# Joint attention scores as two 288-key pieces with a full-height mask matmul, and the third group's attention ordered ahead of weight splitting

## The chip, the cores and the metric

The kernel runs on one core of a Trainium2 chip. The time is device microseconds of that core for one execution, the median of several. An execution that was recorded by the hardware profiler gives the trace; its span is counted from the first instruction to the last.

## What is computed

Causal attention with a decay, for 4 batches of 8 heads (576 positions, 64 numbers per head), and behind it two gated expert layers on the 2304 positions:

```python
def _attn_ref(q, k, v, f):                      # [4, 8, 576, 64], f: [4, 8, 576]
    scores = np.matmul(q, k.transpose(0, 1, 3, 2)) / np.sqrt(D)
    cum = np.cumsum(np.log(np.clip(f, 0.0001, 1.0)), axis=-1)
    scores = np.where(causal, -1e9, scores + cum[:, :, :, None] - cum[:, :, None, :])
    attn = np.exp(scores - np.max(scores, axis=-1, keepdims=True))
    return np.matmul(attn / (np.sum(attn, axis=-1, keepdims=True) + 1e-09), v)

x = attn_out.transpose(0, 2, 1, 3).reshape(2304, 512)
xn = x / np.sqrt(np.mean(x * x, -1, keepdims=True) + 1e-06) * rms_g
x = (silu(xn @ w_gate) * (xn @ w_val)) @ w_out          # 512 -> 1536 -> 512
return (silu(x @ w_gate2) * (x @ w_val2)) @ w_out2
```

## The kernel before

**Precision.** Numbers that need more than one pass are kept as a rounded high part and a remainder (called hi and lo). A product in the expert layers is three matmuls: hi by hi, hi by lo, lo by hi (lines 1758 to 1760). Splitting a 128x512 weight tile is a cast on ScalarE or VectorE (lines 307 and 309) and a subtraction on GpSimd or VectorE (line 312).

**Groups.** The 2304 positions are worked on in four groups of 512 to 640. Groups 1 and 2 (`GROUPS` with kind 0) hold the first 256 positions of the batches, groups 3 and 4 (kind 1) the remaining 320 of batches 0, 1 and of 2, 3. While the expert layers of one group run on TensorE, the attention of the next one is worked in between: group 3's beside the expert layers of group 2 (from 278.8 us), group 4's beside those of group 3 (from 544.3 us). The last group's expert layers are computed with a seven-product scheme (from line 1380 and 1472 on).

**Weights.** A group's expert layers use 72 weight tiles, 12 matmuls of 512 columns each. The first group converts them, splits them and stores the unsplit ones. The second group's `fetch` loads them again, splits them, and stores the split form to memory (the DMA on line 1735); the third group loads the split form (line 1727). Eleven tiles are there at most at a time, so loads and splits run ahead of TensorE by as many.

**One pair of heads of kind 1** (`pair_wide`, `wide_part`). Two heads are worked on together in three parts. Part 0 has 128 queries against 384 keys, part 1 the next 128 against 512, each head in a PSUM bank of its own. Part 2, the *joint* part, has the last 64 queries of both heads, 64 rows for each, against all 576 keys: the operands of one head are zero in the rows of the other, and both accumulate into the same bank. Since a bank holds 512 columns, the keys go in two pieces, 512 and 64. Each piece is four matmuls, for each of two heads a 128-row one (line 810: hi and lo of queries against hi of keys) and a 68-row one (line 811: remainders and decay). At the end of a part a mask matmul adds a large negative number above the diagonal: a constant triangle times the identity, accumulated onto the last 128 columns (line 817) or, in the joint part, onto the 64-column piece, where only 64 rows of the constants are used (line 815).

Then VectorE takes the maximum of each piece (line 828) and of the two, ScalarE the exponential with its sum (line 846), one of three engines the scaling (867, 869), TensorE the transposes (919), ScalarE or VectorE the split of the transposed weights (307, 309, 931), and TensorE the product with the values (947). A pair's keys and queries are loaded and split before that by `head_kq` (616 to 626 and 307, 312), its values by `head_v`.

**What sets the order.** The program is written out by a list scheduler (`Plan`) before it runs. Each piece of work is a generator with a priority; the scheduler estimates when every next operation could start on each engine, and takes the one with the earliest start; among those within 0.01 us of each other the lowest priority number goes first. The order on each engine is then fixed. Priorities: weights 2 plus the tile's number times 0.0001 (`W_PRIO`); attention `A_PRIO`, one number for each half of each group (the third group's are the fifth and sixth: 2.5 and 4.2), its loads and splits 0.2 lower; evacuation of expert layers near 0; expert matmuls 5 and more. A pair of the third group may start when the second group's expert layers have reached a given tile (`UNIT_SPREAD`: the first head at tile 4 and one every 4 tiles, the second half from tile 32).

**What the change touches.** The constant `A_PRIO` (line 88), and in `wide_part` the plan of pieces (792), the mask matmul (815), the slices of the exponentials (840, 845). The tile `dC`, which takes the exponentials, has 576 columns before and after.

Of the kernel before, what the change touches and what calls it, by code (L numbers as in the profile page):

```python
# [17 lines left out]
B, H, S, D = 4, 8, 576, 64  # L18
# [17 lines left out]
NCH = (2, 5)  # L36
NMAX = max(QN)
NW, NL = 512, 384

COLS = ((0, 256), (0, 256), (128, 448), (0, 320))  # L40
LEFT_OVER = COLS[2][0] + NW
# [43 lines left out]
H_PSUM = [lambda h: h % 4 == 0, lambda h: True, lambda h: True]  # L85
MB = 2
W_PRIO = 2
A_PRIO = (3, 4, 4.1, 4.1, 2.5, 4.2, 4.2, 0.5)
W_FREE = 0
A16, D16, S16 = 0.885, 0.485, 0.485  # L90
W_EARLY, W_FIRST = 4.5, 7
# [140 lines left out]
def pe(n):  # L232
    return max(0.107, n / 2400 + 0.0135)
# [18 lines left out]
def actp(n):  # L252
    return n / 1200 + 0.168
# [10 lines left out]
def op(eng, dur, fn, *deps):  # L264
    return Op(((eng, dur, 0.0),), lambda e: fn(), deps)
# [12 lines left out]
def tile_attention_moe_moe(  # L278
# [13 lines left out]
    nc = tc.nc  # L292
# [43 lines left out]
    mir = sb.tile([P, 4, P], F32R, name="mir")  # L336
# [418 lines left out]
    def pair_wide(hds, before, started, done):  # L755


        hd = hds[0]
        kind, s = hd.kind, hd.slots
        yield wait(before, hds[0].kq_ready, hds[1].kq_ready)  # L760
        st, e0 = yield Take(s["tm"], ())
        hl, e1 = yield Take(s["p"], (e0,))
        scored, scaled, split_, out_ = [], [], [], [[], []]
        n = 3 if kind else 2
        ev = [{x: Event() for x in ("scored", "scaled", "split")} for _ in range(n)]
        for i in range(n):
            spawn(wide_part(hds, i, st, hl, ev[i], Event(max(e0.t, e1.t))), plan.current[1])
        yield wait(*(x["scored"] for x in ev))
        last = Event(max(x["scored"].t for x in ev))
        for x in hds:  # L770
            x.kq_drop(last)
        later(started, last)
        yield wait(*(x["scaled"] for x in ev))
        s["tm"].give(st, Event(max(x["scaled"].t for x in ev)))
        both_ = []
        for i, x in enumerate(hds):
            both_.append(Event())
            spawn(wide_values(x, i, hl, [e for y in ev for e in (y["split"],)], both_[i], done[i]), plan.current[1])
        yield wait(*both_)
        s["p"].give(hl, Event(max(e.t for e in both_)))  # L780

    def wide_part(hds, part, st, hl, ev, e0):
        hd = hds[0]
        kind, s = hd.kind, hd.slots
        joint = part == 2
        kn = ((128, 256), (384, 512, 576))[kind][part]
# [2 lines left out]
        tok, e1 = yield Take(sc_tokens[hd.style], ())  # L789

        if joint:
            plan_ = (((0, 1), 0, 512, 0),), (((0, 1), 512, D, 0),)
        elif kind:
            plan_ = (((0,), 0, kn, 0),), (((1,), 0, kn, 0),)
        else:
            plan_ = (((0,), 0, kn, 0), ((1,), 0, kn, kn)),
        sc, es = [], []
        for groups in plan_:
            bank, eb = yield Take(banks, ())

            def mm():
                for heads, k0, m, col in groups:
                    o = bank[:, col : col + m]
                    first = True
                    for x in heads:
                        k1, kb, q1, qb = hds[x].kq
                        qs = slice(320 - D * x, 448 - D * x) if joint else slice(q0, q0 + P)
                        ks = slice(k0, k0 + m)
                        last = k0 + m < kn and x == heads[-1]
                        nc.tensor.matmul(o, q1[:, qs], k1[:, ks], start=first, stop=False)  # L810
                        nc.tensor.matmul(o, qb[:, qs], kb[:, ks], start=False, stop=last)  # L811
                        first = False
                    if k0 + m == kn:
                        if joint:
                            nc.tensor.matmul(o, mir[:D, 3], mir[:D, 1, :D], start=False, stop=True)
                        else:
                            nc.tensor.matmul(bank[:, col + kn - P : col + kn], mir[:, 0], mir[:, 1], start=False, stop=True)

            cost = sum(2 * len(h) * pe(m) for h, _, m, _ in groups) + pe(P)
            e = yield op("PE", cost, mm, hds[0].kq_ready, hds[1].kq_ready, e0, e1, eb)  # L820
            sc.append(bank)
            es.append(e)
        later(ev["scored"], es[-1])
        c = 8 * part
        for i, (bank, e) in enumerate(zip(sc, es)):
            if kind:
                m = plan_[i][0][2]
# [8 lines left out]
        dt, e1 = yield Take(s[("dA", "dB", "dC")[part]], ())  # L836
        ex = []
        for i in range(2):
            if joint:
                o, src, b = dt[:, 512 * i : 512 + D * i], sc[i][:, : (512, D)[i]], 0  # L840
            else:
                o, b = dt[:, kn * i : kn * (i + 1)], i
                src = sc[i][:, :kn] if kind else sc[0][:, kn * i : kn * (i + 1)]
            ex.append((yield op(
                "ACT", actp(kn if not joint else (512, D)[i]) + 0.3,
                lambda: nc.scalar.activation(
                    o, src, AF.Exp, scale=0.125, bias=st[:, c + 2 + b : c + 3 + b], accum_out=st[:, c + 4 + i : c + 5 + i]
                ), em, e1,
            )))
            if kind:  # L850
                banks.give(sc[i], ex[i])
# [10 lines left out]
        for i in range(k):  # L862
            o, m = dt[:, w // k * i : w // k * (i + 1)], st[:, c + 4 + i : c + 5 + i]
# [701 lines left out]
    def attention(g):  # L1565

        for s in range(2):
# [4 lines left out]
            for h, hd in enumerate(heads):  # L1572
# [3 lines left out]
                early = () if g == 0 or at < 0 else (steps[g - 1][max(at - 6, 0)],)  # L1576
                pr = A_PRIO[2 * g + s] + i * 0.001
                if hd.style:
# [426 lines left out]
```

## Time and profile before

| | |
|---|---|
| median of 3 runs | 1082.31 us (1080.14 to 1084.54) |
| profiled execution, span | 1078.3 us (its time outside the span isn't recorded; the median is 4.0 above) |
| instructions | 17640, of them 5584 matmuls |
| VectorE, ScalarE, GpSimd busy | 780.6, 602.4, 452.3 us |
| memory traffic | 193.31 MB read, 86.65 MB written, 260 GB/s |
| granted TensorE clock | 0.995 of 2.4 GHz in the mean |

Matmuls are pipelined: the profile gives each one a duration (0.39 us for 512 columns) that is longer than the distance to the next one's start (0.23 us), and its ends are modelled. What a matmul costs in a row of matmuls is therefore read from the starts. A row `L810 PE MATMUL bank<-k,q 128*128 128x512` is a matmul of line 810 with 128 rows of contraction, 128 columns of weights and a moving operand of 512 columns.

### The profile page before, as it was taken

What the parts mean: (1) busy time and instruction counts of PE and PEld (TensorE: products, weight loads), DVE (VectorE), ACT (ScalarE), POOL (GpSimd) and SP (SyncE); (2) the same over time, 40 slices, a digit from 0 to 9 for tenths busy, and PEclk for the clock granted to TensorE, in tenths of its full rate; (3) what the DMA queues carried; (4) which work ended last, traced back from release to release, by engine and by line L of the source; (5) the groups of instructions that cost most, each with busy time, mean ns of one, the idle gap of its engine ahead of it and who ended that gap; (6) DMA issues with size and microseconds to landing.
All of it is one profiled execution on the core that took longest, in us unless ns stands there. A gap on an engine that the chain in (4) does not pass through costs nothing.

```text
span 1078.3 us, 17640 instructions
## 1 busy us (share of the span) xinstructions
PE 1068.1 (99%) x5584; PEld 943.6 (88%) x5584; DVE 780.6 (72%) x1634; ACT 602.4 (56%) x1326; POOL 452.3 (42%) x484
## 2 busy tenths in 40 slices
PE   8999999999999999999999999999999999999998
PEld 8888888888888888888888888888889999999998
DVE  6878888888455657776647766777776878788773
ACT  6776768775556664776325565555643335543352
POOL 0321302324356666658325774657823340244310
PEclk9989999999999999999999999999999999999999
DMA  7846799775997776775899899997895557755583
GB/s 212 259 163 219 265 310 309 231 257 161 366 399 258 241 243 228 252 248 205 303 374 363 303 347 377 340 339 264 326 333 168 196 186 244 234 179 169 193 260 109
DMA packets 136497, 281.21 MB, mean 261 GB/s; under 512 B 14674, under 2 KB 57490, under 8 KB 136402
## 3 DMA queue, kind: packets, MB, share of 16 engines
q1 hardware_dynamic: 136404, 280.09, 75.7%
q8 instruction: 44, 0.72, 0.3%
q14 instruction: 49, 0.40, 0.1%
HBM read 193.31 MB, written 86.65 MB: 260 GB/s over the span
## 4 chain that ended last, share of the span: by engine, by line
PE 96%; DMA 1%; DVE 1%; POOL 1%; issue 0%; ACT 0%; POOLq 0%; DVEq 0%; SPq 0%
PE bank L1758 18%; PE bank L1759 18%; PE bank L1760 18%; PE bank L1472 5%; PE bank L1474 5%; PE bank L1473 5%; PE bank L947 3%; PE bank L919 3%; PE bank L1381 3%; PE bank L1382 3%; PE bank L1380 3%; PE bank L810 2%; PE bank L811 2%; PE bank L667 2%; PE bank L720 2%; PE bank L704 1%
## 5 line engine op out<-in xcount | busy, mean ns | idle before, releaser
L312 POOL TENSOR_TENSOR whl<-w,whl 128x512 fp32r<-128x512 f32 x119 | 157.8, 1329 | 216.4 <-ACT whl L307 170.3
L1758 PE MATMUL bank<-X,whl 128*128 128x512 f32 x564 | 227.3, 403 | 0.0
L1759 PE MATMUL bank<-X,whl 128*128 128x512 f32 x564 | 220.7, 391 | 0.0
L1760 PE MATMUL bank<-X,whl 128*128 128x512 f32 x564 | 220.3, 391 | 0.0
L307 ACT CAST whl<-w 128x512 fp32r<-128x512 f32 x178 | 108.7, 617 | 38.5 <-PE bank L1759 15.5
L1760 PEld LDWEIGHTS bank<-X,whl 128*128 128x128 f32 x564 | 106.2, 188 | 23.3
L1758 PEld LDWEIGHTS bank<-X,whl 128*128 128x128 f32 x564 | 106.3, 188 | 20.6
L1759 PEld LDWEIGHTS bank<-X,whl 128*128 128x128 f32 x564 | 106.5, 189 | 18.9
L1758 PE MATMUL bank<-H,whl 128*128 128x512 f32 x215 | 87.4, 407 | 0.0
L1760 PE MATMUL bank<-H,whl 128*128 128x512 f32 x215 | 84.9, 395 | 0.0
L1759 PE MATMUL bank<-H,whl 128*128 128x512 f32 x215 | 84.9, 395 | 0.0
L1900 ACT ACTIVATE tmp<-bank 128x384 f32<-128x384 f32 x48 | 23.6, 492 | 92.0 <-DVE bank L1510 91.2
L1890 ACT ACTIVATE tmp<-bank 128x512 f32<-128x512 f32 x72 | 43.1, 599 | 50.6 <-PE bank L1760 49.4
L1892 DVE SCALAR_TENSOR_TENSOR tmp<-tmp,bank 128x512 f32<-128x512 f32 x72 | 49.3, 684 | 25.4 <-ACT tmp L1890 23.6
L1913 DVE SCALAR_TENSOR_TENSOR bank<-tmp,bank 128x512 f32<-128x512 f32 x60 | 41.6, 694 | 32.5 <-PE bank L1760 32.3
L312 DVE TENSOR_TENSOR whl<-w,whl 128x512 fp32r<-128x512 f32 x78 | 54.5, 705 | 11.8 <-ACT whl L307 11.1
L828 DVE TENSOR_REDUCE tm<-bank 128x1 f32<-128x512 f32 (+1 forms) x96 | 50.4, 560 | 15.0 <-PE bank L811 7.9
L931 DVE TENSOR_TENSOR pl<-bank,ph 128x512 fp32r<-128x512 f32 (+1 forms) x80 | 49.9, 631 | 8.7 <-ACT ph L307 8.3
L1695 POOL TENSOR_SCALAR w<-w,rebase 128x512 f32<-128x512 f32 x19 | 18.0, 951 | 88.3 <-DMA w<-w 84.1
L1712 DVE SCALAR_TENSOR_TENSOR w<-w,wk 128x512 int32<-128x512 int32 x72 | 52.9, 742 | 1.4 <-ACT wk L1701 1.1
L312 POOL TENSOR_TENSOR kb<-raw,k 64x576 fp32r<-64x576 f32 x31 | 44.4, 1432 | 19.5 <-ACT k L307 18.1
L1473 PE MATMUL bank<-X,whl 128*128 128x384 f32 x154 | 51.4, 334 | 0.0
(306 smaller groups left out, 2815.9 us busy)
## 6 DMA issues: line engine op xcount, KB each, us to landing
whl<-w_split SPq DMA_DIRECT2D x90, 512.0 KB
w<-w SPq DMA_DIRECT2D x72, 512.0 KB
w<-w_f SPq DMA_DIRECT2D x144, 256.0 KB
w_split<-whl SPq DMA_DIRECT2D x72, 512.0 KB
w_f<-w SPq DMA_DIRECT2D x72, 256.0 KB
w_sums<-w SPq DMA_DIRECT2D x48, 256.0 KB
w_sums_split<-whl SPq DMA_DIRECT2D x23, 512.0 KB
w<-w_sums SPq DMA_DIRECT2D x41, 256.0 KB
```

The source lines that it names most:

```text
L307: nc.scalar.copy(o, i)
L312: (nc.vector if e == "DVE" else nc.gpsimd).tensor_tensor(o, a, b, op=ALU.subtract)
L828: em = yield op("DVE", dve(m), lambda: nc.vector.tensor_reduce(st[:, c + i : c + i + 1], bank[:, :m], axis=AX.X, op=ALU.max), e)
L931: e = yield op("DVE", dve(n), lambda: nc.vector.tensor_tensor(low, src, o.bitcast(F32), op=ALU.subtract), e)
L1472: nc.tensor.matmul(o, w[:, 0, cs], xh, start=c == 0, stop=False)
L1473: nc.tensor.matmul(o, w[:, 0, cs], xl, start=False, stop=False)
L1474: nc.tensor.matmul(o, w[:, 1, cs], xh, start=False, stop=c == 1)
L1712: lambda: nc.vector.scalar_tensor_tensor(ti, ti, 3, k, op0=ALU.logical_shift_left, op1=ALU.bitwise_or), e, et,
L1758: nc.tensor.matmul(o, wh[:, cs], xh, start=start, stop=False)
L1759: nc.tensor.matmul(o, wh[:, cs], xl, start=False, stop=False)
L1760: nc.tensor.matmul(o, wl[:, cs], xh, start=False, stop=stop)
L1892: "DVE", dve(n), lambda: nc.vector.scalar_tensor_tensor(a, a, 1.0, b, op0=ALU.add, op1=ALU.mult), e,
```

## The change

The joint part's two pieces become equal: 288 and 288 keys. The mask matmul uses all 128 rows of the constants (the identity's rows from 64 on are zero in the 64 columns used, so these rows add nothing) and is accumulated onto the last 64 columns of the second piece. Maximum and exponential are taken of 288 columns twice. The third group's attention gets the priority 1.9 in both halves, below the weights' 2.

```diff
+JOINT = S // 2
-A_PRIO = (3, 4, 4.1, 4.1, 2.5, 4.2, 4.2, 0.5)
+A_PRIO = (3, 4, 4.1, 4.1, 1.9, 1.9, 4.2, 0.5)
@@ wide_part
-            plan_ = (((0, 1), 0, 512, 0),), (((0, 1), 512, D, 0),)
+            plan_ = (((0, 1), 0, JOINT, 0),), (((0, 1), JOINT, JOINT, 0),)
...
-                            nc.tensor.matmul(o, mir[:D, 3], mir[:D, 1, :D], start=False, stop=True)
+                            nc.tensor.matmul(o[:, m - D :], mir[:, 3], mir[:, 1, :D], start=False, stop=True)
...
-                o, src, b = dt[:, 512 * i : 512 + D * i], sc[i][:, : (512, D)[i]], 0
+                o, src, b = dt[:, JOINT * i : JOINT * (i + 1)], sc[i][:, :JOINT], 0
...
-                "ACT", actp(kn if not joint else (512, D)[i]) + 0.3,
+                "ACT", actp(JOINT if joint else kn) + 0.3,
```

## Rows read from the trace of the kernel before

**Rows 1.** The page: busy us of each engine, share of the span, instructions.

```profile
PE 1068.1 (99%) x5584; PEld 943.6 (88%) x5584; DVE 780.6 (72%) x1634; ACT 602.4 (56%) x1326; POOL 452.3 (42%) x484
```

**Rows 2.** The page: the chain that ended last, by engine.

```profile
PE 96%; DMA 1%; DVE 1%; POOL 1%; issue 0%; ACT 0%; POOLq 0%; DVEq 0%; SPq 0%
```

**Rows 3.** Waits of TensorE: for whom, us in total, times, longest.

```profile
...
PE bank L919 <- POOL dB L869: 1.1, 1, 1.1
PE bank L919 <- POOL dA L869: 0.4, 1, 0.4
...
```

**Rows 4.** Line 815: count, duration in ns, first and last start, forms.

```profile
L815 PE MATMUL bank<-mir x16: 294/294/294, 320.5 to 769.7; 64*128 64x64 f32 x16
```

**Rows 5.** Timeline of TensorE, one joint part: start us, us, instruction.

```profile
692.01 0.39 PE L810 MATMUL bank<-k,q 128*128 128x512 f32 x1
...
692.47 0.40 PE L810 MATMUL bank<-k,q 128*128 128x512 f32 x1
...
692.94 0.20 PE L810 MATMUL bank<-k,q 128*128 128x64 f32 x1
...
693.09 0.28 PE L810 MATMUL bank<-k,q 128*128 128x64 f32 x1
693.20 0.28 PE L811 MATMUL bank<-kb,qb 68*128 68x64 f32 x1
693.40 0.29 PE L815 MATMUL bank<-mir 64*128 64x64 f32 x1
...
693.96 0.39 PE L1759 MATMUL bank<-X,whl 128*128 128x512 f32 x1
694.19 0.39 PE L1760 MATMUL bank<-X,whl 128*128 128x512 f32 x1
```

**Rows 6.** Timeline of TensorE, parts 0 and 1 of the same pair.

```profile
687.12 0.33 PE L810 MATMUL bank<-k,q 128*128 128x384 f32 x1
...
687.48 0.22 PE L817 MATMUL bank<-mir 128*128 128x128 f32 x1
...
689.46 0.40 PE L1759 MATMUL bank<-X,whl 128*128 128x512 f32 x1
```

**Rows 7.** Groups by shape, lines 828 and 846: busy us, mean ns, idle before.

```profile
L828 DVE TENSOR_REDUCE tm<-bank 128x1 f32<-128x512 f32 x48 | 32.6, 683 | 8.0 <-PE bank L811 7.9
L828 DVE TENSOR_REDUCE tm<-bank 128x1 f32<-128x384 f32 x32 | 16.4, 549 | 7.0 <-PE bank L817 7.0
...
L828 DVE TENSOR_REDUCE tm<-bank 128x1 f32<-128x64 f32 x16 | 3.4, 213 | 0.0
...
L846 ACT ACTIVATE dC<-bank,tm 128x512 f32<-128x512 f32 x16 | 11.1, 693 | 0.2 <-DVE tm L835 0.2
...
L846 ACT ACTIVATE dC<-bank,tm 128x64 f32<-128x64 f32 x16 | 5.0, 311 | 0.0
```

**Rows 8.** Tile dC: its transposes, first and last start.

```profile
L919 PE MATMUL bank<-mi,dC x80: 270/272/273, 328.5 to 780.4; 128*128 128x128 f32 x64, 128*64 128x128 f32 x16
```

**Rows 9.** Line 1735: the stores of split weights, first and last start.

```profile
L1735 SPq DMA_DIRECT2D w_split<-whl x72: 319/327/1312, 272.5 to 520.0; - x72
```

**Rows 10.** Timeline of TensorE where the second and third group's expert layers begin.

```profile
278.77 0.39 PE L1758 MATMUL bank<-X,whl 128*128 128x512 f32 x1
...
543.60 0.40 PE L1758 MATMUL bank<-late_h,whl 128*128 128x512 f32 x1
...
544.30 0.40 PE L1758 MATMUL bank<-X,whl 128*128 128x512 f32 x1
```

**Rows 11.** Groups of GpSimd by shape from 278 to 545 us: preparation of heads.

```profile
L312 POOL TENSOR_TENSOR kb<-raw,k 64x576 fp32r<-64x576 f32 x15 | 21.4, 1427 | 5.8 <-ACT k L307 5.5 <-DMA w_split<-whl 0.2
L312 POOL TENSOR_TENSOR v<-rv,v 128x320 fp32r<-128x320 f32 x16 | 14.2, 890 | 5.3 <-ACT v L307 4.9
L312 POOL TENSOR_TENSOR q<-raw,q 64x256 fp32r<-64x256 f32 x16 | 11.9, 746 | 4.6 <-ACT q L307 3.5
```

**Rows 12.** Stretch of the third group's expert layers: busy us by engine, PEclk, DMA.

```profile
545.00:812.00 267.00, 265.44 (x1325) 223.01 (x1324) 189.89 (x426) 144.04 (x352) 153.90 (x180) 1.00 0.93 335
```

## The prediction

> **What bounds the kernel now.** I read the page's busy line first. TensorE has a matmul in flight for 99% of the span, the next engine for 72% [rows 1]. Matmul ends are modelled, so I asked next whether the starts wait for anything. The chain of waits says no: 96% of it is matmul following matmul [rows 2]. Of the few entries in the list of what matmuls waited for, two lie in the stretch in which the joint parts run, 1.1 and 0.4 us, both for a scaling on GpSimd [rows 3]. So from the second group on, the time is the sum of the steps from one matmul's start to the next, and an edit is worth what it takes out of these steps, as long as it makes no new wait.
>
> **The change, part by part.** The joint part runs 16 times (its mask matmul on line 815 is counted 16 times, from 320.5 to 769.7 us [rows 4]).
>
> *The joint part's length now.* I take it from its first matmul to the second expert matmul behind it, because a short matmul shifts part of its cost into the step after the next start. 692.01 to 693.96 is 1.95 us; one step of an undisturbed 512-column matmul (693.96 to 694.19, 0.23) belongs to the expert matmul, so the joint part holds TensorE for 1.72 us [rows 5]. Inside it: a pair of 512-column matmuls, one with 128 rows and one with 68, steps 0.46 to 0.47 (692.01 to 692.47 to 692.94). The 64-column matmuls step 0.11 each (693.09 to 693.20), although they have an eighth of the columns. Two pairs at 0.47 and four at 0.11 make 1.38, and the mask matmul on 64 rows is left with 0.34: 0.20 before it starts (693.20 to 693.40) and a late follower.
>
> *The price of a mask matmul of full height.* The two parts before the joint one hold two pairs of 384 columns, two pairs of 512 and four full-height masks of 128 columns. From 687.12 to the second expert matmul at 689.46 it is 2.34, less 0.23, so 2.11 [rows 6]. A 384 pair takes 0.36 (687.12 to 687.48), a 512 pair 0.47; 2.11 - 0.72 - 0.94 = 0.45, or 0.11 per mask, the same as a 64-column matmul [rows 5, 6].
>
> *Mask edit.* 0.34 becomes 0.11: 0.23 less, 16 times, 3.7 us. A full-height mask of 64 columns has no row. It may be as cheap as nothing, wholly hidden behind its neighbours, or as dear as the present 0.34. I take 0.11, since the two nearest kinds agree on it.
>
> *Score edit.* Two 512 pairs and two 64 pairs become four pairs of 288 columns. No row has 288. From 384 columns (0.36) to 512 (0.47) a pair grows by 0.11 in 128 columns; 96 columns fewer than 384 take off 0.08, so I take 0.28. The bounds: a pair can't be cheaper than two 64-column steps (0.22), nor dearer than a 384 pair (0.36). Four pairs: 1.12 (0.88 to 1.44) against 1.38 now, so 0.26 less, 16 times 4.2 us (between 8.0 gained and 1.0 lost).
>
> *Sum.* 1.72 - (1.12 + 0.11) = 0.49 us each, 16 x 0.49 = 7.8 us. With both ends of both prices: from -1.0 (dear pairs, mask unchanged) to 8.0 + 16 x 0.34 = 13.4 us.
>
> A rule of the Trainium skill speaks against the score edit: in "TensorE: Matmul & The Clock Gate", section "Back-to-back issue gap", a warm isolated matmul is put at N/2.4 + 2.5 ns. Both versions stream 2304 columns in eight score matmuls, so by it the edit is worth nothing and the sum is 3.7. The trace is near it at 512 columns (0.23 us [rows 5] against 0.216) and far off at 64 (0.11 against 0.029), so I go by the trace.
>
> *VectorE and ScalarE.* Reduce and exponential are split 288 + 288 instead of 512 + 64. Reduces take 0.683, 0.549 and 0.213 us for 512, 384 and 64 columns; exponentials 0.693 and 0.311 for 512 and 64 [rows 7]. Both are close to straight lines in the columns, so two of 288 cost what 512 and 64 cost together (0.896 and 1.004): nothing, and neither engine is the bound. What moves is the order inside: the last reduce, which runs when TensorE has left the part, grows from 0.21 to some 0.43 (between the 64 and 384 rows). So the joint part's weights are ready 0.2 us later against TensorE. That is covered: from the mask at 320.5 [rows 4] to the first transpose of these weights at 328.5 [rows 8] lie 8 us of other matmuls, and no wait on them stands in the list [rows 3].
>
> *The order edit.* The third group's attention (eight pairs of heads) goes ahead of the weight splitting on ScalarE, VectorE, GpSimd and the DMA queue. The list scheduler decides by it only between pieces that could start within 0.01 us of each other. Its gain: TensorE doesn't wait in that stretch, so nothing. Its cost: split weights come later. The first is sent to its store at 272.5 [rows 9] and used at 278.8 [rows 10], 6.3 us of lead; the last is stored at 520.0 [rows 9] and its 12 matmuls, at 0.233 each (543.60 to 544.30 are three), end at 544.30 [rows 10], so it is used from 541.5, with 21 us of lead. A head's preparation puts 1.43 + 0.89 + 0.75 = 3.1 us on GpSimd [rows 11], 6.2 us for a pair; were a split to stand behind a whole pair, it would still be in time, and with VectorE (72% busy [rows 1]) as the second engine for splits. I cost it at nothing. If the cover is gone, it shows at the first pairs, by 2 to 5 us in all. The loads of heads and weights share one queue, issued in the scheduler's order; in the busiest stretch, behind 545 us, the 16 DMA engines are at 0.93 [rows 12] and the shorter joint parts squeeze that by 8 x 0.49 of 267 us, 1.5%, to 0.94, which still holds. The waits of 1.1 and 0.4 may go or return elsewhere: 1.5 us either way.
>
> **The sum against the times.** 1078.3 of span less 7.8 is 1070.5. The runs' median of 1082.3 lies 4.0 above the span; that stays, so I predict 1074.5 us.
>
> **Rivals.**
> 1. *Columns alone set the steps* (the rule above as a mechanism of this kernel: the 0.11 of a 64-column step is an effect of this place, not of its size, and comes back in the 288 steps). Only the mask edit pays: 1082.3 - 3.7 = 1078.6. For it: 288 has no row. Against it: the steps of 0.11 [rows 5]. 5%.
> 2. *The mask stays dear* because what costs is its place at the end of a group, not its 64 rows. Then 1082.3 - 4.2 = 1078.1. Against it: full-height masks close a group too, at 0.11 [rows 6]. 5%.
> 3. *The order edit and the new plan make waits.* TensorE's order is fixed beforehand; a transpose that meets a scaling not yet done stops everything behind it. One such wait is 1.1 us [rows 3]; four or five more give back 5 us: 1079.5. For it: every queue's order from the second group on is planned anew. Against it: only two such waits among 16 pairs now. 10%.
> 4. *Slower.* The same stop, but built into the joint part: if the later second reduce lets the transposes of dC come before their scaling in all 16 parts, at 1.1 us each it is 17.6 us, and 1082.3 - 7.8 + 17.6 = 1092.1. It eats the gain from seven such parts on, and is a measurable loss from 12. Against it: the 8 us of other matmuls between [rows 4, 8]. 6%.
> 5. *More than forecast*: pairs near 0.24 (16 x 4 x 0.04 = 2.6 us more) and both present waits gone (1.5): 1070.4. 6%.
>
> **How the numbers follow.** The forecast has the remaining 68%, with its own range 1072 to 1077 (a pair between 0.25 and 0.31, waits 1.5 up or down). A measurement of this kernel can tell 0.5%, 5.4 us, from no change, so faster means below 1076.9: the forecast nearly whole (66%), case 5 (6%), a fifth of case 3: 74%. Within 0.5%: cases 1 and 2, most of 3, the edge of the forecast: 20%. Slower: 6%. The range 1070 to 1079.5 leaves out case 4 and some of 3 and 5.
>
> **What would show it.** Lines 810 and 811 should have only 288-column forms in the joint part, 64 matmuls on each line, stepping 0.28 a pair; the joint part should hold TensorE for 1.2 us by the same reading; the mask should be a 128-row form and its follower start within 0.1. The span should lose what the 16 parts lose. The prediction is wrong if a 288 pair steps 0.32 or more, if the expert matmul behind the mask still comes 0.3 late, or if the list of TensorE's waits between 280 and 812 us grows past 4 us; a first split weight that TensorE waits for soon after 278.8 us would convict the order edit.

## The result and the profile after

Five runs of each, the changed kernel at a median of 1069.59 us (1067.01 to 1071.79), the kernel before at 1082.31 (1075.94 to 1085.31): ratio 0.9914, interval 0.9886 to 0.9942. The ratio is the record's own estimate with its 95% interval; the quotient of these two medians is 0.988, just outside it, and the record doesn't show what makes the difference. Measured again in a later set the ratio was 0.9932 (0.9910 to 0.9953), with medians of 1071.26 and 1077.81, 6.6 us apart. The profiled execution after took 1071.79 us with a span of 1070.0.

The span fell by 8.3 us, but not all of that is the change's. The first 280 us have the same order of instructions on all engines before and after (the first difference is a load issued at 280.3), and yet the second group's expert layers begin 1.7 us earlier in this execution. Over all profiles of this study that moment lay between 274.0 and 283.6 us. So I compare from there on. These are the rows of TensorE's timeline after for the begin of the second, third and fourth group's expert layers and for the last matmul:

```profile
277.06 0.39 PE L1759 MATMUL bank<-X,whl 128*128 128x512 f32 x1
...
540.65 0.39 PE L1759 MATMUL bank<-X,whl 128*128 128x512 f32 x1
...
804.04 0.34 PE L1473 MATMUL bank<-X,whl 128*128 128x384 f32 x1
...
1066.00 0.34 PE L1383 MATMUL bank<-h11h,whl 128*128 128x384 f32 x1
```

Before, the first two are in [rows 10], and the other two are these:

```profile
812.32 0.33 PE L1472 MATMUL bank<-X,whl 128*128 128x384 f32 x1
...
1074.27 0.34 PE L1382 MATMUL bank<-h11h,whl 128*128 128x384 f32 x1
```

The second group's stretch went from 265.5 to 263.6 us, the third's from 268.0 to 263.4, the last group's stayed at 262.0. Together 795.5 became 788.9: 6.6 us.

A joint part after, read as in [rows 5] (TensorE's timeline: start us, us, instruction):

```profile
712.52 0.29 PE L811 MATMUL bank<-k,q 128*128 128x288 f32 x1
712.65 0.30 PE L812 MATMUL bank<-kb,qb 68*128 68x288 f32 x1
712.78 0.30 PE L811 MATMUL bank<-k,q 128*128 128x288 f32 x1
712.92 0.30 PE L812 MATMUL bank<-kb,qb 68*128 68x288 f32 x1
713.05 0.29 PE L811 MATMUL bank<-k,q 128*128 128x288 f32 x1
...
713.46 0.30 PE L812 MATMUL bank<-kb,qb 68*128 68x288 f32 x1
713.59 0.20 PE L816 MATMUL bank<-mir 128*128 128x64 f32 x1
713.62 0.47 PE L1759 MATMUL bank<-X,whl 128*128 128x512 f32 x1
713.94 0.40 PE L1760 MATMUL bank<-X,whl 128*128 128x512 f32 x1
714.17 0.39 PE L1761 MATMUL bank<-X,whl 128*128 128x512 f32 x1
```

A pair steps 0.26 to 0.27, the mask's follower starts 0.03 behind it, and 712.52 to 713.94 less one step of 0.23 is 1.19 us, against 1.72 before. That is 0.53 us in each of 16 parts, 8.5 us. Of the 1.19, the four pairs take 1.07 (712.52 to 713.59) and the mask 0.12 (713.59 to 713.94 less 0.23).

The chain's first line and TensorE's waits on scalings after (answering [rows 2, 3]; waits: us in total, times, longest):

```profile
PE 86%; DMA 8%; POOL 2%; DVE 1%; issue 1%; ACT 0%; SPq 0%; POOLq 0%; ACTq 0%; DVEq 0%
```

```profile
PE bank L920 <- POOL dA L870: 1.5, 2, 1.1
PE bank L920 <- POOL dB L870: 0.6, 1, 0.6
PE bank L920 <- POOL dC L870: 0.3, 1, 0.3
```

The chain now leaves TensorE where it follows such a wait back. The list counts only what it can ascribe. To count all, I took every step from one matmul's start to the next and subtracted the shortest step with the same succession of four shapes; what exceeds it by over 0.06 us I call waiting; steps taken at a lower clock count in it too. By that the second and third group's stretches waited 2.4 us before and 4.0 after, and without waits they came down from 531.2 to 523.0, which is 8.2. So: 8.2 taken out of the steps, 1.6 given back in waits.

The smaller readings: reduce and exponential by shape (busy us, mean ns, idle before), and the stores of split weights (count, ns, first and last start):

```profile
L829 DVE TENSOR_REDUCE tm<-bank 128x1 f32<-128x288 f32 x32 | 14.4, 452 | 6.6 <-PE bank L812 5.6
```

```profile
L847 ACT ACTIVATE dC<-bank,tm 128x288 f32<-128x288 f32 x32 | 15.8, 496 | 1.2 <-DVE tm L836 1.2
```

```profile
L1736 SPq DMA_DIRECT2D w_split<-whl x72: 319/342/1417, 270.8 to 517.3; - x72
```

Two reduces are 0.90 us and two exponentials 0.99, as before. The split weights keep their lead: 277.06 - 270.8 = 6.3 us at the first, as before.

### The profile page after: what moved, and what is told of

It reads as the page before. It is cut to its first block, busy times and chain, and to the rows that moved or that the text cites. A ratio compares the mean times of both kernels' runs of the same rounds, so it can differ in the third digit from the quotient of the medians.

```text
span 1070.0 us, 17663 instructions
## 1 busy us (share of the span) xinstructions
PE 1058.7 (99%) x5584; PEld 937.4 (88%) x5584; DVE 778.8 (73%) x1640; ACT 599.8 (56%) x1320; POOL 450.7 (42%) x484
## 4 chain that ended last, share of the span: by engine, by line
PE 86%; DMA 8%; POOL 2%; DVE 1%; issue 1%; ACT 0%; SPq 0%; POOLq 0%; ACTq 0%; DVEq 0%
PE bank L1759 16%; PE bank L1760 16%; PE bank L1761 16%; PE bank L1474 5%; PE bank L1473 5%; PE bank L1475 5%; DMA w<-w_f 3%; PE bank L1383 3%; PE bank L1382 3%; PE bank L1381 3%; PE bank L948 3%; PE bank L920 3%; PE bank L668 2%; PE bank L721 2%; PE bank L811 2%; PE bank L812 2%
## 5 line engine op out<-in xcount | busy, mean ns | idle before, releaser
L308 ACT CAST whl<-w 128x512 fp32r<-128x512 f32 x173 | 105.6, 618 | 37.8 <-PE bank L1760 9.7
L1759 PE MATMUL bank<-H,whl 128*128 128x512 f32 x211 | 85.2, 404 | 0.0
L1760 PE MATMUL bank<-H,whl 128*128 128x512 f32 x211 | 83.3, 395 | 0.0
L1761 PE MATMUL bank<-H,whl 128*128 128x512 f32 x211 | 83.3, 395 | 0.0
L829 DVE TENSOR_REDUCE tm<-bank 128x1 f32<-128x384 f32 (+2 forms) x96 | 51.7, 561 | 9.9 <-PE bank L812 5.6
L1474 PE MATMUL bank<-X,whl 128*128 128x384 f32 x150 | 50.1, 334 | 0.0
L1473 PE MATMUL bank<-X,whl 128*128 128x384 f32 x150 | 50.1, 334 | 0.0
```

Of the source, the lines that this page charges most:

```text
L308: nc.scalar.copy(o, i)
L829: em = yield op("DVE", dve(m), lambda: nc.vector.tensor_reduce(st[:, c + i : c + i + 1], bank[:, :m], axis=AX.X, op=ALU.max), e)
L1473: nc.tensor.matmul(o, w[:, 0, cs], xh, start=c == 0, stop=False)
L1474: nc.tensor.matmul(o, w[:, 0, cs], xl, start=False, stop=False)
L1759: nc.tensor.matmul(o, wh[:, cs], xh, start=start, stop=False)
L1760: nc.tensor.matmul(o, wh[:, cs], xl, start=False, stop=False)
```

## The experiments

One table for all. "Stretch" is from the second group's first expert matmul to the last matmul; joint part, waits and the sum of groups two and three without waits are read as above. Ratios come from all executions of a set, the other columns from one profiled execution of each kernel. In the experiments, the distance between the median and that of before in the same set agrees within 1.3 us with what the stretch gained, except in 7 and 12, where the medians gained 1.2 and 4.2 us and the profiled stretches -1.9 and 0.4.

| kernel | ratio to before (interval) | stretch us | joint us | waits us | without waits us |
|---|---|---|---|---|---|
| before | | 795.5 | 1.72 | 2.4 | 531.2 |
| changed | 0.9914 (0.9886 to 0.9942) | 788.9 | 1.19 | 4.0 | 523.0 |
| 1 order alone | 1.0017 (0.9996 to 1.0039) | 795.1 | 1.72 | 2.2 | 531.0 |
| 2 mask of 64 rows | 0.9977 (0.9955 to 0.9998) | 791.3 | 1.50 | 1.5 | 527.9 |
| 3 pieces 512 and 64 | 0.9970 (0.9947 to 0.9992) | 791.7 | 1.50 | 1.9 | 527.8 |
| 4 order of before | 0.9966 (0.9939 to 0.9992) | 792.6 | 1.19 | 7.7 | 523.0 |
| 5 changed again | 0.9932 (0.9910 to 0.9953) | 789.1 | 1.19 | 4.2 | 522.9 |
| 6 old priorities | 1.0004 (0.9979 to 1.0030) | 796.8 | 1.19 | 12.1 | 522.8 |
| 7 preparation first | 0.9993 (0.9969 to 1.0016) | 797.4 | 1.19 | 11.8 | 523.6 |
| 8 second half only | 0.9929 (0.9908 to 0.9951) | 789.5 | 1.19 | 4.9 | 522.7 |
| 9 slack 1.0 | 0.9910 (0.9878 to 0.9941) | 785.6 | 1.19 | 0.5 | 523.1 |
| 10 slack 1.0 again | 0.9899 (0.9868 to 0.9930) | 786.2 | 1.19 | 1.2 | 523.1 |
| 11 slack 2.0 | 0.9926 (0.9904 to 0.9949) | 787.4 | 1.19 | 2.3 | 523.1 |
| 12 slack 1.0, old priorities | 0.9969 (0.9945 to 0.9993) | 795.1 | 1.19 | 9.7 | 523.5 |

**1. The order edit alone.**

```diff
-A_PRIO = (3, 4, 4.1, 4.1, 2.5, 4.2, 4.2, 0.5)
+A_PRIO = (3, 4, 4.1, 4.1, 1.9, 1.9, 4.2, 0.5)
```

> The kernel before with the third group's attention priority alone at 1.9 in both halves; pieces 512 and 64, mask on 64 rows as before. Theory (the order edit is worth nothing, the gain is the shorter joint part): within 2 us of the kernel before, waits of TensorE on scalings between 280 and 812 us of 1 to 4 us in all, joint part at 1.72 us. Rival (the order edit made the new waits of 1.1 and 0.7 us near 420 and 430 us seen in the changed kernel): the second group's expert layers take 2 us longer than the 265.5 us of before. Second rival (part of the gain is the order edit's): 2 us or more faster than before.

The same as before in every column. By itself the order edit is worth nothing.

**2. The changed kernel with the mask on 64 rows.** TensorE's order is the changed kernel's.

```diff
-nc.tensor.matmul(o[:, m - D :], mir[:, 3], mir[:, 1, :D], start=False, stop=True)
+nc.tensor.matmul(o[:, m - D :], mir[:D, 3], mir[:D, 1, :D], start=False, stop=True)
```

> The changed kernel with the mask matmul on 64 rows again, still onto the last 64 columns of the second 288-key piece; the order of all engines is the changed kernel's. Theory (64 rows are what made the mask dear): the joint part goes from 1.19 to about 1.42 us, 16 x 0.23 = 3.7 us more than the changed kernel. Rival (the mask was dear because it followed 64-column matmuls): unchanged within 0.5 us over groups two and three.

TensorE's timeline around one mask:

```profile
338.22 0.30 PE L812 MATMUL bank<-kb,qb 68*128 68x288 f32 x1
338.45 0.29 PE L816 MATMUL bank<-mir 64*128 64x64 f32 x1
338.67 0.50 PE L1759 MATMUL bank<-X,whl 128*128 128x512 f32 x1
339.01 0.39 PE L1760 MATMUL bank<-X,whl 128*128 128x512 f32 x1
```

It starts 0.23 after its forerunner and holds its follower for another 0.22, where the full-height one takes 0.13 and 0.03. That is 0.31 us per part, more than the 0.23 expected; 16 times it is 5.0, and the column without waits shows 4.9. The 64 rows are the cause, not the place behind 64-column matmuls. The Trainium skill says in "TensorEngine Tiling (Array Packing)", section "Tiling Modes", that a change of tiling mode drains the engine; the trace fits that, with a gap on both sides of the only matmul of that height, but no run here tells a drain from another cause of the gaps.

**3. The changed kernel with pieces of 512 and 64 and the full mask.** The scheduler got the 288-column costs, so TensorE's order is the changed kernel's.

```diff
-JOINT = S // 2
+JOINT, WIDE = S // 2, 512
...
-plan_ = (((0, 1), 0, JOINT, 0),), (((0, 1), JOINT, JOINT, 0),)
+plan_ = (((0, 1), 0, WIDE, 0),), (((0, 1), WIDE, S - WIDE, 0),)
...
```

> The changed kernel with pieces of 512 and 64 keys and the full-height mask; the scheduler is given the 288-column costs, so the order of TensorE is the changed kernel's. Theory (64-column matmuls step 0.11 because of their size): the joint part goes from 1.19 to about 1.45 us, 16 x 0.26 = 4.2 us more. Rival (columns alone set the steps): unchanged within 0.5 us.

TensorE's timeline of the short piece:

```profile
335.13 0.27 PE L812 MATMUL bank<-kb,qb 68*128 68x64 f32 x1
335.24 0.28 PE L811 MATMUL bank<-k,q 128*128 128x64 f32 x1
335.35 0.28 PE L812 MATMUL bank<-kb,qb 68*128 68x64 f32 x1
335.46 0.28 PE L816 MATMUL bank<-mir 128*128 128x64 f32 x1
335.58 0.48 PE L1759 MATMUL bank<-X,whl 128*128 128x512 f32 x1
```

0.11 a step for 64 columns, beside 0.13 for 288 in the changed kernel. The part is at 1.50 us, 4.8 us more in the sum without waits, where 4.2 was expected. Columns alone don't set the steps. In the stretch, experiments 2 and 3 lost only 2.4 and 2.8 us against the changed kernel: with TensorE slower in the same order, its waits fell from 4.0 to 1.5 and 1.9.

**4. The new joint part in the order of before.** Pieces of 288 and the full mask, planned with the costs of 512 and 64 and the old priorities.

```diff
-NW, NL = 512, 384
-JOINT = S // 2
+NW, NL, JOINT, PLANNED = 512, 384, S // 2, (512, 64)
...
-cost = sum(2 * len(h) * pe(m) for h, _, m, _ in groups) + pe(P)
+cost = sum(2 * len(h) * pe(PLANNED[gi] if joint else m) for h, _, m, _ in groups) + pe(P)
```

(and the same for the reduce and the exponential)

> The kernel before with 288-key pieces and the full-height mask, planned with the costs of 512 and 64 and the old priorities, so that the order of TensorE is that of before. Theory: the joint part is at 1.19 us and the kernel about 8 us faster than before, with waits of TensorE like those of before (2 us) or 1 to 2 us more because the scalings come no earlier while TensorE does. Rival (the new order pays for part of the gain): less than 6 us faster than before.

The joint part is as short as in the changed kernel, the sum without waits the same 523.0, but 7.7 us of waits leave 2.9 of the 8.2. The order of instructions is that of before on every engine. Of the waits that the list names in this stretch, all but one of 0.2 us are on scalings or on VectorE's work just before them (us in total, times, longest):

```profile
PE bank L919 <- POOL dA L869: 2.7, 2, 1.5
...
PE bank L919 <- POOL dB L869: 1.4, 1, 1.4
PE bank L919 <- DVE tm L859: 0.8, 1, 0.8
PE bank L919 <- ACT dA L867: 0.5, 1, 0.5
```

TensorE got quicker, the scalings didn't, and its fixed order meets them too early. The theory's 1 to 2 us of waits more was wrong; the rival held. The medians of this set, 3.6 us apart, agree with the 2.9.

**5. The changed kernel again.**

> The changed kernel unaltered, again. Theory (the first 280 us vary from execution to execution, what follows doesn't): from the second group's first expert matmul to the last matmul 788.9 us within 1 us, as in its first profile, whatever the span; 0.5 to 0.7% faster than the kernel before on the same chip. Rival (the 4 us of waits on scalings are chance): they move by 2 us or more between the two profiles.

The stretch and the waits repeat within 0.2 us. The two largest waits of the first profile, 1.3 and 0.7 us, are back at the same places with 1.2 and 0.8 (423.1 and 431.8 for 421.3 and 430.0, 1.8 us later, as the second group's begin is by 1.9). These belong to the order, not to the execution. The rest, 2.0 us in one and 2.3 in the other, is not the same: 0.5 at 575.2 is gone, and a wait for a split that was 0.3 at 675.3 is 1.0 at 677.3. That the sums agree so well is partly chance.

```profile
PE bank L1760 <- DVE X L313: 0.8, 1, 0.8
```

**6. The change without the order edit.**

```diff
-A_PRIO = (3, 4, 4.1, 4.1, 1.9, 1.9, 4.2, 0.5)
+A_PRIO = (3, 4, 4.1, 4.1, 2.5, 4.2, 4.2, 0.5)
```

> The changed kernel with the third group's old priorities 2.5 and 4.2; pieces of 288, full mask, planned with their own costs. Theory (the order edit is worth nothing): from the second group's first expert matmul to the last matmul 788.9 us within 2 us; joint part 1.19 us. Rival (the order edit is needed for the scalings to be in time): waits in groups two and three as in the kernel with the order of before (7.7 us) instead of 4.0, so 792 us or more. Second rival (the order edit made the waits of group two): 787 us or less.

No gain is left: 796.8 us, which misses the theory and lies in the first rival's range, though for another reason than the scalings. TensorE's timeline and the stretches (us, busy by engine, granted clock, DMA) where the third group's expert layers begin:

```profile
524.65 0.20 PE L816 MATMUL bank<-mir 128*128 128x64 f32 x1
...
547.46 0.80 PE L1759 MATMUL bank<-X,whl 128*128 128x512 f32 x1 [4.73 <-ACT X L308]
548.12 0.80 PE L1760 MATMUL bank<-X,whl 128*128 128x512 f32 x1
...
550.00 0.63 PE L1761 MATMUL bank<-X,whl 128*128 128x512 f32 x1
550.42 0.63 PE L1759 MATMUL bank<-X,whl 128*128 128x512 f32 x1
```

```profile
540.00:547.50 7.50, 2.77 (x13) 1.93 (x11) 4.48 (x15) 1.03 (x3) 2.87 (x3) 0.95 0.87 287
547.50:554.00 6.50, 6.50 (x16) 4.88 (x17) 4.15 (x10) 1.48 (x4) 2.45 (x4) 0.54 0.22 84
554.00:570.00 16.00, 16.00 (x72) 13.25 (x71) 8.31 (x15) 6.00 (x14) 5.88 (x7) 1.00 0.98 341
```

TensorE waits 4.7 us for the group's normalized input, and behind the idle stretch the granted clock is 0.54 for 6.5 us, near the lower of its two levels (1.2 of 2.4 GHz): 512 columns step 0.43 instead of 0.23, which adds some 3 us. Together that is 8.0 of the 12.1 us of waits; the other 4.1 are about as many as in the changed kernel. The way back: the last mask of this attention (the first row, at 524.65) lies 22.8 us before that begin, in the changed kernel 32.6, in the kernel before 30.7. And the last head's keys are loaded 228.5 us after the second group's begin (the first row below: 508.36 - 279.89), against 205.1 in the changed kernel (the second row: 482.12 - 277.06) and 213.0 before.

```profile
508.36 0.45 SPq L617 DMA_DIRECT2D raw<-qk  x1
```

```profile
482.12 0.33 SPq L617 DMA_DIRECT2D raw<-qk  x1
```

**7. Only the preparation of heads goes first.** Old attention priorities, but loads and splits of the third group's keys, queries and values at 1.7.

```diff
-spawn(head_kq(hd, go[0], *early), pr - 0.2)
+spawn(head_kq(hd, go[0], *early), 1.7 + i * 0.001 if g == 2 else pr - 0.2)
```

(and the same for `head_v`)

> 288-key pieces, full mask and the old attention priorities 2.5 and 4.2, but the loads and splits of the third group's keys, queries and values alone at 1.7, as the change gives them. Theory (the scores with old priorities lost their gain because the last heads' preparation stood behind weight loads and splits, so that the third group's input came late): no wait at the start of the third group's expert layers, from the second group's first expert matmul to the last matmul 789 us within 1. Rival (the attention itself, its exponentials and scalings, has to go ahead): the wait stays, 794 us or more.

Half right. The wait at the third group's begin is gone, the last mask lies 33.3 us ahead of it: the late preparation was what made the input late. But 11.8 us of waits stand elsewhere, most of those that the list names on scalings (7.2 us), and the time is no better.

```profile
PE bank L920 <- POOL dA L870: 4.1, 4, 1.8
...
PE bank L920 <- ACT dA L868: 2.0, 4, 0.8
...
PE bank L920 <- ACT dB L868: 1.1, 2, 0.6
```

Some 1.6 of the 11.8 are again steps at the lower clock: behind a wait of 2.0 us on a scaling at 580.9 the granted clock is 0.67 in the mean until 586.0.

**8. The second half of the third group's attention alone at 1.9** (2.5 for the first).

> The changed kernel with the priority 1.9 for the second half of the third group alone, 2.5 for the first. Theory (the deadline is the end of the second half): no wait at the start of the third group's expert layers, 789 us within 2. Rival (both halves are needed): a wait of 2 us or more there.

As good as the changed kernel, with no wait at the third group's begin: the new priority of the second half is enough. Of its 4.9 us of waits some 1.5 are steps at the lower clock behind a wait of 1.8 us at 601.6 (0.64 in the mean from 601.2 to 606.0).

**9 to 11. Slack for the scalings.** The scheduler is told that a scaled tile is ready 1.0 us later (2.0 in the third) than it thinks, for the transposes alone.

```diff
-e = yield op("PE", len(parts) * 0.109, mm, e0, e1, ready)
+e = yield op("PE", len(parts) * 0.109, mm, e0, e1, Event(ready.t + SLACK))
```

> The changed kernel with the scheduler told that a scaled tile is ready 1.0 us later than it thinks, for the transposes alone. Theory (the 4.0 us of waits come from transposes placed in TensorE's order ahead of a scaling that runs late): waits in groups two and three under 1.5 us, from the second group's first expert matmul to the last matmul 786 us. Rival (they come from engines that are short of time, so the wait moves elsewhere): 788 us or more.

> The changed kernel with slack of 1.0 us before the transposes, again. Theory: 785.6 us from the second group's first expert matmul to the last matmul within 0.5, 0.7 to 1.0% faster than the kernel before. Rival (its lead over the changed kernel was the first 280 us of one execution): no better than the changed kernel's 0.9932.

> The same with 2.0 us. Theory: no waits of TensorE on scalings of 0.3 us or more, 785 to 786 us; if 2 us is too much, the values' products and the pairs behind come late and TensorE waits for keys or weights instead.

With 1.0 us the waits fall to 0.5 and 1.2 us and the stretch to 785.6 and 786.2, 3 us below the changed kernel, 9 to 10 below before. All waits that the list names for TensorE in the first of these runs are now on lines that run ahead of the second group's stretch:

```profile
PE bank L389 <- DVE H L376: 3.3, 1, 3.3
PE bank L747 <- DVE tmp L736: 2.4, 2, 1.5
PE bank L668 <- DMA qk<-cum: 0.5, 1, 0.5
```

So the waits came from transposes placed too early, not from engines short of time. The repeat at 1.0 us has one wait on a scaling again (0.5 in the list), and its stretch and its gain of 1.01% lie just outside what was expected of it. With 2.0 us the waits on scalings stay away, but 0.9 us for the split of transposed weights and 0.7 for queries come instead, and the stretch is 787.4, not 785 to 786. The two runs at 1.0 are the fastest measured (0.9910 and 0.9899), but their intervals overlap with that of the changed kernel; its lead of 3 us is shown by the traces.

**12. Slack of 1.0 with the old priorities.**

> Slack of 1.0 us before the transposes with the old priorities 2.5 and 4.2. Theory (slack takes the waits on scalings away, the order edit the late input; they are two things): a wait of some 5 us and a half-clock stretch at the start of the third group's expert layers, waits on scalings under 1 us, 792 us or so. Rival (slack alone does it): 786 us.

The late input is there again, with 2.5 us of waiting where some 5 were expected, then steps of 0.43. There are 4.8 us of other waits in the third group's stretch, 1.4 of them on a scaling, so that the scalings stayed not quite under the 1 us expected. The stretch is 795.1 us for 792 or so; the medians, 4.2 us below before, are nearer to what was expected than this one profile. The order edit and the slack are two things.

## Why the prediction was right, point by point

*What bounds the kernel*: right. Without waits, groups two and three take 522.7 to 523.6 us in all ten profiles with the new joint part, 531.0 to 531.2 with the old one, whatever the order. An edit is worth what it takes out of the steps, less the waits it makes.

*Mask and score edits*: 0.49 us forecast, 0.53 measured, 1.19 us a part for 1.23. The 288 pair came to 0.27 for 0.28. The 0.04 is the pairs': four took 1.07 us for 1.12, the mask 0.12 for 0.11. Each edit was sized well where it stands alone against the old part (experiments 2 and 3 are the other corners of that square: 1.72 to 1.50 by either), 0.23 for the mask as forecast (experiment 3) and 0.22 for the scores' 0.26 (experiment 2). Together they give 0.53, 0.08 more than the two alone: the 64-row mask costs 0.31 more than the full one behind the 288-column pairs and 0.23 more behind the 64-column ones. Adding the two edits leaves that out; the prices of the new part, from which the same 0.49 comes, don't need it.

*VectorE and ScalarE at nothing*: right; the reduce is 0.452 for 0.43, and the DMA engines are at 0.94 in the third group's stretch, as forecast.

*The order edit at nothing*: this step failed. Alone it is worth nothing (experiment 1), and I priced it against the trace of before, where the third group's input is in time. But the score edit has the whole program planned anew, and in that plan the old priorities bring the last heads' keys 23 us later than the new ones (experiment 6). Beside the score edit the order edit is worth 796.8 - 789.0 = 7.8 us, as much as the step saving (6.6 us between the medians of experiments 5 and 6). I asked only whether its own cost was covered; what I missed is that the other edit moves the deadline and the order, so that the two can't be priced apart. With the order edit in, the stretch lost 6.6 us of the 7.8 forecast.

*The waits, 1.5 us either way*: 1.6 up. The list names 2.4 us between 280 and 812, below the 4 that would have spoken against the prediction, and no wait on a split weight. Rival 3 happened in its mildest form. Rivals 1 and 2 fell with experiments 3 and 2; rival 4 didn't happen: one wait of 0.3 us on the tile `dC` is listed.

*The sum against the times*: the span was forecast at 1070.5 and came at 1070.0, partly by luck, since 1.7 us of it is the execution's start. The 1074.5 made from it was 4.9 too high: the median of 1069.6 lies below the forecast's own 1072 to 1077 and 0.4 below the whole range. By the ratio, 0.9914 of 1082.3, it would be 1073.0, inside both. 0.5 of the 4.9 is the span. 2.2 is in the 4.0 around the span: every execution on record has only 1.7 to 1.9 outside it (after: 1071.79 to 1070.0), and the rest was the distance from the profiled execution to the median of others. The last 2.2 is that the execution profiled after was the slowest of its five. The 1082.3 was high as well: in three later sets of 28 to 35 executions the kernel before has medians of 1077.8 to 1078.7. So of the 12.7 us between the first two medians about half is chance, and 6.6 is the change.

What stays open: why the plan of experiment 7 has so many waits on scalings. Each kernel here is one plan; that new priorities are better in general isn't shown, only that the late input comes with the old ones in both plans made with the costs of the 288-column pieces and nothing moved ahead (6 and 12), and not with the new ones. Planned with the old costs (4), the old priorities bring no late input.

## What to carry to other kernels

On an engine that hardly waits, price an edit by the distance from start to start, and let both ends of a short instruction in: its cost stands partly in the step of its follower. Where a scheduler orders the program from estimated times, an edit that makes the bound engine faster can make it meet unfinished work, as here in experiment 4; compare the sum without waits and the waits apart, try some slack in the estimate where the order is fixed (1.0 us paid here, 2.0 less), and don't price an edit of priorities against the old plan when another edit plans anew.

## What was not expected of the hardware

A matmul of 64 rows among matmuls of 68 and 128 rows costs 0.31 us more than one of 128 rows with the same 64 columns, in gaps of 0.1 before and 0.2 behind it; 68 rows beside 128 cost nothing of the kind (0.13 a step for either in the changed kernel).

The first 57 us differ between executions of the same order, with the granted clock; here for experiments 5 and 9 (stretch: us, busy by engine, clock, DMA):

```profile
0.00:57.00 57.00, 52.09 (x379) 49.90 (x379) 40.61 (x111) 39.82 (x99) 10.14 (x24) 0.96 0.79 232
```

```profile
0.00:57.00 57.00, 50.70 (x391) 48.55 (x392) 42.23 (x114) 41.11 (x104) 10.98 (x26) 1.00 0.77 229
```

At 1.00 twelve more matmuls have begun by 57 us than at 0.96, and the second group begins at 275.1 instead of 278.9. The 0.96 is a mean: in experiment 5 the granted clock is 0.50, the lower level of 1.2 GHz, from 51.9 to 62.1 us, where TensorE begins 42 matmuls; in experiment 9 it stays at 1.00 there and 72 begin. Both have a wait for the same work just before, of 1.4 us until 49.4 and of 1.5 until 50.2, so that the wait alone doesn't tell whether the clock falls; what does is not shown.

That is where most of the spread of this kernel's times is. From TensorE's 391st matmul to the second group's begin it is 218.1 to 219.3 us in all fourteen profiles, but the 391st starts between 55.8 and 65.4, 9.6 us apart; the 35 times of the kernel before in one set lie 9.4 apart. For an edit of under 1% the stretch of a profile, which repeated within 0.2 and 0.6 us here, tells more than a median of five.
